# The last output tile of an attention and feed-forward kernel: other column parts, a bank for each, other engines for their copies and sends

## The chip, the core and the metric

The kernel runs on one core of a Trainium2 chip. The metric is the device time of one execution in microseconds; lower is better. A core has a matrix engine (TensorE), three engines for elementwise work (VectorE, ScalarE, GpSimd) and a queue engine (SyncE, SP in the profile). TensorE writes its results to PSUM, an on-chip memory of banks; VectorE or ScalarE copies them from there to SBUF, and a DMA sends them from SBUF to the output in HBM.

## The reference

Linear attention with the feature map phi, and then a gated feed-forward block on its output. Batch is 8, heads 8, sequence 576, head width 64; there are 4608 tokens of width 512, and the hidden width is 1536.

```python
def phi(x):
    return np.where(x > 0, x, np.exp(x) - 1.0) + 1.0

q_p, k_p = phi(q), phi(k)
kv  = einsum('bhsd,bhse->bhde', k_p, v)
z   = sum(k_p, axis=2)
num = einsum('bhsd,bhde->bhse', q_p, kv)
den = einsum('bhsd,bhd->bhs', q_p, z)[..., None] + 1e-06
x   = (num / den), heads side by side: 4608 x 512
g   = x @ w_gate
out = (g * sigmoid(g) * (x @ w_val)) @ w_out          # 4608 x 512, float32
```

## The kernel before

The tokens are worked through in NG = 9 groups of 512. For each group, layer 1 (`l1`, line 292 for the matmuls) makes the hidden activations `hT` in FB = 12 blocks of 128 hidden units: two products into a pair of PSUM banks, a silu on ScalarE and a multiplication on VectorE. Layer 2 then makes the output in four tiles t = 0 to 3 of 128 tokens by 512 columns. Each is a sum over the 12 hidden blocks: `l2_mm` (line 299) is one matmul of that sum, with the weights of one `hT` block loaded and 512 columns of `w_out` streamed. `l2_open` gives the tile its PSUM bank, `l2_out` copies the finished bank to an SBUF tile `osb`, on ScalarE (through the helper at line 120) or on VectorE (line 322), and sends it to HBM in two halves of 64 tokens (line 326), e = 0 and e = 1.

All of PSUM is four pairs of banks, held in the list `ring`. `pair()` takes the pair at the front of the list and puts it at the end, so that a pair comes round again after three others. `l2_open` takes a new pair for tiles 0 and 2; tiles 1 and 3 use the second bank of the pair. The order of the instructions on each engine is the order in which the code issues them. Waits between engines are derived from the tiles and banks that the instructions use. Each queue (SP's, ScalarE's) issues its sends in order.

The last tile, g = 8 and t = 3, is done apart (lines 737 to 744): its 512 columns go in two parts, 0 to 384 and 384 to 512, one after the other, each with its own 12 matmuls. Both parts lie in one bank. The first is copied by VectorE, and both of its halves are sent from SP's queue. The second is copied by ScalarE; its first half is sent from SP's queue and its second half from ScalarE's. The tiles before it are copied by ScalarE (t = 0), VectorE (t = 1) and ScalarE (t = 2), and are sent from SP's queue. At the program's end (line 774) SP waits until all sends have landed.

Of the kernel before, what the change touches and what calls it, by code (L numbers as in the profile page):

```python
# [17 lines left out]
def kernel(  # L18
# [10 lines left out]
    nc = tc.nc  # L29
# [9 lines left out]
    NG = B * J // U  # L39
# [53 lines left out]
    def pair(p=None):  # L93
        i = 0 if p is None else [x is p for x in ring].index(True)
        p = ring.pop(i)
        ring.append(p)
        return p
# [8 lines left out]
    def ld2(src, dst, b):  # L106
        ld(src, dst, b, 0)
        ld(src, dst, b, 1)
# [10 lines left out]
    def act(out, in_, func=AF.Copy, scale=1.0, bias=0.0):  # L119
        nc.scalar.activation(out=out, in_=in_, func=func, bias=bias, scale=scale)  # L120
# [15 lines left out]
    def exp_k(b, lp):  # L136
        act(jl(ek, b, lp), lj(kr, b, lp), AF.Exp)

    def exp_q(b, lp):
        act(eq[b % 2][:, hs(lp), :], qr[b % NB][:, hs(lp), :], AF.Exp)  # L140
# [26 lines left out]
    def phi_k(b, lp):  # L167
        mx_k(b, lp)
        mn_k(b, lp)
        add_k(b, lp)  # L170
# [19 lines left out]
    def kv_all(b):  # L190
        kvp[b] = pair()
        for lp in range(2):
            kv_corner(b, lp, kp, True, True)
# [9 lines left out]
    def zsum(b, l0=0, l1=2):  # L203
        a, z = kp[b % 2][:, l0:l1, :, :], zs[:, l0:l1, :, :]
        nc.vector.tensor_tensor(out=z[:, :, 0:4, :], in0=a[:, :, 0:4, :], in1=a[:, :, 4:8, :], op=ALU.add)
        nc.vector.tensor_tensor(out=z[:, :, 0:2, :], in0=z[:, :, 0:2, :], in1=z[:, :, 2:4, :], op=ALU.add)
        nc.vector.tensor_tensor(out=z[:, :, 0, :], in0=z[:, :, 0, :], in1=z[:, :, 1, :], op=ALU.add)
        nc.vector.tensor_tensor(out=z[:, :, 0, :], in0=z[:, :, 0, :], in1=a[:, :, 8, :], op=ALU.add)
# [31 lines left out]
    def units(g):  # L240
        us = [(u // J, u % J) for u in range(U * g, U * g + U)]
        res = []
        for b in sorted(set(u[0] for u in us)):
            js = [j for (bb, j) in us if bb == b]
            res.append((b, js[0], js[-1] + 1, C * us.index((b, js[0]))))
        return us, res
# [26 lines left out]
    def l1_mm(g, fb, ps, chunks):  # L273
        for c in chunks:
            for h, w in enumerate((wg, wv)):
                nc.tensor.matmul(out=ps[h][:, :], lhsT=w[:, c, P * fb:P * fb + P], rhs=xT[g % 2][:, c, :],  # L276
                                 start=(c == 0), stop=(c == 3))
# [3 lines left out]
    def l1_post(g, fb, ps):  # L281
        s = sil[sn[0] % 4]
        sn[0] += 1
        act(s[:, :], ps[0][:, :], AF.Silu)
        nc.vector.scalar_tensor_tensor(out=hT[g % 2][:, fb, :], in0=ps[1][:, :], scalar=SC,  # L285
                                       in1=s[:, :], op0=ALU.mult, op1=ALU.mult)

    def l1(g, fb):
        ps = pair()
        for h, w in enumerate((wg, wv)):  # L290
            for c in range(4):
                nc.tensor.matmul(out=ps[h][:, :], lhsT=w[:, c, P * fb:P * fb + P], rhs=xT[g % 2][:, c, :],  # L292
                                 start=(c == 0), stop=(c == 3))
        l1_post(g, fb, ps)

    l2p = {}
# [5 lines left out]
    def l2_open(g, t):  # L302
        if t % 2 == 0:
            l2p[(g, "p", t // 2)] = pair()
        l2p[(g, t)] = l2p[(g, "p", t // 2)][t % 2]

    def lay2(g, t):
        l2_open(g, t)
        for fb in range(FB):
            l2_mm(g, t, fb)  # L310
# [3 lines left out]
    def l2_out(g, t, eng, n0=0, n1=512, o=None):  # L314
        if o is None:
            o = osb[on[0] % 4]
            on[0] += 1
        ps = l2p[(g, t)]
        if eng == "A":
            act(o[:, n0:n1], ps[:, n0:n1], scale=1.0 / SC)  # L320
        else:
            nc.vector.tensor_scalar(out=o[:, n0:n1], in0=ps[:, n0:n1], scalar1=1.0 / SC, scalar2=None, op0=ALU.mult)  # L322
        for e in range(2):
            b, j = units(g)[0][2 * t + e]
            dma = nc.scalar if g == NG - 1 and t == 3 and n1 == 512 and e == 1 else nc.sync
            dma.dma_start(out=out[S * b:S * b + S, n0:n1].rearrange("(c j) f -> j c f", j=J)[j],
                              in_=o[C * e:C * e + C, n0:n1])
        return o
# [196 lines left out]
    def none():  # L525
        return [[] for _ in range(FB)], [[] for _ in range(4)]

    def lam(f, *a):
        return lambda: f(*a)
# [19 lines left out]
    def period0():  # L549
        sl, w = none()  # L550
        b = 1
        sl[7] = [lam(mx_k, b, 0), lam(exp_q8), lam(exp_k, b, 0), lam(phi_q8), lam(mn_k, b, 0), lam(add_k, b, 0)]
        sl[8] = [lam(zsum, b, 0, 1)]
        sl[10] = [lam(mx_k, b, 1)]
        return sl

    def chain(b, at):
        return {
            at: [lam(s3_prod, b, 0)],
            at + 1: [lam(s3_reduce, b, 0), lam(s3_recip, b, 0)],  # L560
            at + 2: [lam(s3_scale, b, 0), lam(dtr, b, 0)],
            at + 3: [lam(s3_prod, b, 1)],
            at + 4: [lam(s3_reduce, b, 1), lam(s3_recip, b, 1)],
            at + 5: [lam(s3_scale, b, 1), lam(dtr, b, 1)],
        }
# [102 lines left out]
    for g in range(NG):  # L668
        b1, b2 = g + 1, g + 2
        if g == 0:  # L670
            sl = period0()
        else:
            sl, _ = none()
            late = []
            if g == 1:
                sl[1] = [lam(zsum, b1)]
                sl[4] = [lam(phi_q, b1, 0)]
                sl[5] = [lam(phi_q, b1, 1), lam(zb, b1)]
                ch = chain(b1, 6)
                late = ch.pop(10) + ch.pop(11)  # L680
            elif b1 < B:
                sl[0] = [lam(phi_q, b1, 0)]
                sl[1] = [lam(phi_q, b1, 1)]
                ch = chain(b1, 2)
            else:
                ch = {}
            for f, v_ in ch.items():
                sl[min(f, FB - 1)] += v_
        for fb in range(FB):
            if g == 0:  # L690
                if fb < 2:
                    continue
                if fb == 4:
                    ld2(k, kr, 2)
                    ld2(q, qr, 2)
                    ld2(v, vr, 2)
            if g == 1 and fb < 2:
                if fb == 0:
                    two = [pair(), pair()]
                    for cs in ((0, 1), (2, 3)):  # L700
                        for i in range(2):
                            l1_mm(g, i, two[i], cs)
                l1_post(g, fb, two[fb])
            else:
                l1(g, fb)
            for f in sl[fb]:
                f()
        if g + 3 < B:
            if g > 0:
                nc.gpsimd.tensor_copy(out=gate[:, :], in_=qT[b1 % 2][:, 1, J - 1, 1, C - 1:C])  # L710
            ld2(k, kr, g + 3)
            ld2(v, vr, g + 3)
            if g > 0:
                ld2(q, qr, g + 3)
        if g == 0:
            layer2_0()
            ld2(q, qr, 3)
        else:
            for f in late:
                f()  # L720
            for t in range(4):
                if t == 0 and b2 < B:
                    if g == 1:
                        nc.scalar.preload_act_table_set("natural_log_exp_and_others")
                    exp_k(b2, 0)
                    exp_k(b2, 1)
                    exp_q(b2, 0)
                    exp_q(b2, 1)
                    phi_k(b2, 0)
                    phi_k(b2, 1)  # L730
                    zsum(b2)
                if t == 1 and g == 1:
                    kv_all(b1)
                    r_copy(b1, 0, 2, "AA")
                if t == 3:
                    block(g)
                if g == NG - 1 and t == 3:
                    l2_open(g, t)
                    o = None
                    for (n0, n1) in ((0, 384), (384, 512)):  # L740
                        for fb in range(FB):
                            l2_mm(g, t, fb, n0, n1)
                        o = l2_out(g, t, "V" if n0 == 0 else "A", n0, n1, o)
                    continue
                lay2(g, t)
                l2_out(g, t, "A" if g == 1 and t == 1 else "AV"[t % 2])
            if b2 < B:
                zb(b2)
# [30 lines left out]
```

## Time and profile before

| | |
|---|---|
| median of 5 runs | 313.65 us |
| lowest and highest | 313.54, 313.74 us |
| the profiled execution's own time | 313.54 us |
| its span in the profile | 311.7 us |
| TensorE busy (PE) | 305.0 us, 98% of the span |
| VectorE busy (DVE) | 205.2 us, 66% |
| ScalarE busy (ACT) | 152.6 us, 49% |
| GpSimd busy (POOL) | 48.4 us, 16% |
| granted TensorE clock | full in all slices of the span |

The span goes from the first to the last instruction of the profiled execution; the execution's own time has about 1.8 us more around it. Times in the profile count from the span's start. A line of the timeline has the start, the length, the engine, the source line, the operation and its output and inputs (`osb<-pp` is a copy from a PSUM bank to an output tile), their shapes, and in brackets the idle time of the engine before it and what ended that. SPq and ACTq are the queues from which SyncE and ScalarE issue their sends; the length of such a line is the time of the issue, not of the transfer.

### The profile page before, as it was taken

What the parts mean: (1) busy time and instruction counts of PE and PEld (TensorE: products, weight loads), DVE (VectorE), ACT (ScalarE), POOL (GpSimd) and SP (SyncE); (2) the same over time, 40 slices, a digit from 0 to 9 for tenths busy, and PEclk for the clock granted to TensorE, in tenths of its full rate; (3) what the DMA queues carried; (4) which work ended last, traced back from release to release, by engine and by line L of the source; (5) the groups of instructions that cost most, each with busy time, mean ns of one, the idle gap of its engine ahead of it and who ended that gap; (6) DMA issues with size and microseconds to landing.
All of it is one profiled execution on the core that took longest, in us unless ns stands there. A gap on an engine that the chain in (4) does not pass through costs nothing.

```text
span 311.7 us, 5565 instructions
## 1 busy us (share of the span) xinstructions
PE 305.0 (98%) x2206; PEld 141.7 (45%) x2206; DVE 205.2 (66%) x361; ACT 152.6 (49%) x231; POOL 48.4 (16%) x73
## 2 busy tenths in 40 slices
PE   7999999999999999999999999999999999999994
PEld 3444454444544454445444544454444444444442
DVE  4755868999599658976697759874981433143410
ACT  4865959448733844374536643574330333033311
POOL 8745444400000510041000500000000000000000
PEclk9999999999999999999999999999999999999999
DMA  8999999999502693239512990323032300240014
GB/s 216 199 197 199 206 207 235 235 206 154 114 11 39 103 195 105 40 60 189 154 38 41 129 236 14 62 53 86 0 76 53 84 1 1 46 91 0 2 34 101
DMA packets 41178, 32.80 MB, mean 105 GB/s; under 512 B 16448, under 2 KB 36160, under 8 KB 41152
## 3 DMA queue, kind: packets, MB, share of 16 engines
q0 software_dynamic: 20480, 18.29, 37.5%
q1 hardware_dynamic: 20592, 14.13, 18.9%
q8 instruction: 17, 0.28, 0.4%
q14 instruction: 9, 0.07, 0.1%
q10 hardware_dynamic: 80, 0.03, 0.0%
HBM read 37.75 MB, written 9.44 MB: 151 GB/s over the span
## 4 chain that ended last, share of the span: by engine, by line
PE 95%; DVE 2%; DMA 1%; SPq 0%; issue 0%; ACT 0%; DVEq 0%
PE pp L292 58%; PE pp L299 30%; PE pp L276 2%; PE pp L254 2%; PE pp L185 2%; DMA q<-in_q_dram 1%; DVE qT L454 1%; PE pp L124 1%; DVE xT L425 0%; PE pp L412 0%; PE pp L212 0%; DVE qp L468 0%; PE pp L374 0%; DVE osb L322 0%; SPq L333 0%
## 5 line engine op out<-in xcount | busy, mean ns | idle before, releaser
L120 ACT ACTIVATE sil<-pp 128x512 f16<-128x512 f32 x108 | 63.4, 597 | 101.0 <-PE pp L292 96.4
L292 PE MATMUL pp<-xT,wg 128*128 128x512 f16 x416 | 106.8, 379 | 0.0
L292 PE MATMUL pp<-xT,wv 128*128 128x512 f16 x416 | 106.8, 379 | 0.0
L285 DVE SCALAR_TENSOR_TENSOR hT<-pp,sil 128x512 f16<-128x512 f32 x108 | 72.2, 680 | 48.0 <-PE pp L292 35.4
L299 PE MATMUL pp<-wo,hT 128*128 128x512 f16 (+2 forms) x444 | 97.1, 373 | 0.6 <-DVE osb L322 0.6
L299 PEld LDWEIGHTS <-hT 128*128 128x128 f16 x444 | 41.9, 98 | 49.9 <-issue 2.1
L292 PEld LDWEIGHTS <-wv 128*128 128x128 f16 x416 | 40.7, 98 | 49.1
L292 PEld LDWEIGHTS <-wg 128*128 128x128 f16 x416 | 40.7, 98 | 48.4
L322 DVE TENSOR_SCALAR osb<-pp 128x512 f32<-128x512 f32 (+1 forms) x19 | 12.9, 681 | 31.1 <-PE pp L299 31.1
L120 ACT ACTIVATE osb<-pp 128x512 f32<-128x512 f32 (+1 forms) x18 | 10.3, 574 | 34.8 <-PE pp L299 30.2
L120 ACT ACT_TABLE_LOAD x13 | 16.7, 1283 | 2.5 <-PE pp L292 2.4
L120 ACT ACTIVATE ek<-kr 128x1152 f16<-128x1152 f16 x16 | 17.8, 1157 | 0.1
L229 DVE TENSOR_TENSOR qp<-qp,rden 128x1152 f16<-128x1152 f16 x12 | 16.2, 1346 | 0.0
L220 DVE TENSOR_REDUCE den<-prod 128x18 f32<-128x1152 f16 x12 | 16.1, 1340 | 0.0
L710 POOL COPY gate<-qT 128x1 f16<-128x1 f16 x4 | 1.1, 281 | 96.1 <-DMA qT<-qp 96.1
L120 ACT ACTIVATE eq<-qr 128x1152 f16<-128x1152 f16 x14 | 15.4, 1151 | 0.0
L271 DVE TENSOR_SCALAR xT<-pp 128x512 f16<-128x512 f32 (+1 forms) x14 | 8.8, 667 | 6.7 <-PE pp L254 6.7
L103 POOL DMA_DIRECT2D vr<-in_v_dram x16 | 11.9, 742 | 8.5 <-DMA wo<-in_moe_w_out_dram 2.4
L103 POOL DMA_DIRECT2D kr<-in_k_dram x16 | 11.6, 725 | 8.7 <-DMA wo<-in_moe_w_out_dram 1.9
L159 DVE TENSOR_TENSOR kp<-ek,kp 128x1152 f16<-128x1152 f16 x15 | 11.4, 758 | 0.5
L147 DVE TENSOR_SCALAR ek<-ek 128x1152 f16<-128x1152 f16 x16 | 7.9, 494 | 5.0 <-ACT ek L120 5.0
L103 POOL DMA_DIRECT2D qr<-in_q_dram x14 | 10.1, 721 | 5.3 <-DMA qr<-in_q_dram 2.3
(86 smaller groups left out, 179.5 us busy)
## 6 DMA issues: line engine op xcount, KB each, us to landing
out_dram<-osb SPq DMA_DIRECT2D x70, 128.0 KB, 2.7
kr<-in_k_dram POOLq DMA_DIRECT2D x16, 288.0 KB, 8.6
vr<-in_v_dram POOLq DMA_DIRECT2D x16, 288.0 KB, 9.5
qr<-in_q_dram POOLq DMA_DIRECT2D x14, 288.0 KB, 11.7
wg<-in_moe_w_gate_dram POOLq DMA_DIRECT2D x5, 256.0 KB, 9.4
wv<-in_moe_w_val_dram POOLq DMA_DIRECT2D x5, 256.0 KB, 9.7
q<-in_q_dram SPq DMA_DIRECT2D x2, 576.0 KB, 3.9
wo<-in_moe_w_out_dram POOLq DMA_DIRECT2D x2, 512.0 KB, 12.4
```

Of the source, the lines that this page charges most:

```text
L103: nc.gpsimd.dma_start(out=dst[b % NB][:, 2 * lp:2 * lp + 2, :], in_=src[b].rearrange("(l a) (c j) d -> (a c) l (j d)", a=2, j=J)[:, 2 * lp ...
L120: nc.scalar.activation(out=out, in_=in_, func=func, bias=bias, scale=scale)
L147: nc.vector.tensor_scalar(out=a, in0=a, scalar1=1.0, scalar2=None, op0=ALU.min)
L159: nc.vector.tensor_tensor(out=a, in0=ek[b % 2][:, lp, :, :], in1=a, op=ALU.add)
L185: nc.tensor.matmul(out=ps[hh][D * l2:D * l2 + D, D * lp:D * lp + D], lhsT=t[b % 2][rows, lp, j, D * l2:D * l2 + D], rhs=vr[b % NB][rows, 2 ...
L220: nc.vector.tensor_reduce(out=den[:, c, :], in_=prod[:, :, :].rearrange("p j (l d) -> p (j l) d", d=D), axis=AX.X, op=ALU.add)
L229: nc.vector.tensor_tensor(out=qv, in0=qv, in1=rden[:, c, :].unsqueeze(2).to_broadcast([P, 2 * J, D]), op=ALU.mult)
L271: nc.vector.tensor_scalar(out=dst, in0=ps[l2][:, c0:], scalar1=1.0 / SC, scalar2=None, op0=ALU.mult)
L285: nc.vector.scalar_tensor_tensor(out=hT[g % 2][:, fb, :], in0=ps[1][:, :], scalar=SC, in1=s[:, :], op0=ALU.mult, op1=ALU.mult)
L292: nc.tensor.matmul(out=ps[h][:, :], lhsT=w[:, c, P * fb:P * fb + P], rhs=xT[g % 2][:, c, :], start=(c == 0), stop=(c == 3))
L299: nc.tensor.matmul(out=l2p[(g, t)][:, n0:n1], lhsT=hT[g % 2][:, fb, P * t:P * t + P], rhs=wo[:, fb, n0:n1], start=(fb == 0), stop=(fb == F ...
L322: nc.vector.tensor_scalar(out=o[:, n0:n1], in0=ps[:, n0:n1], scalar1=1.0 / SC, scalar2=None, op0=ALU.mult)
```

## The change

The last tile is cut at column 320 instead of 384. Each part gets its own PSUM bank: after the first part has been copied, the next pair is taken from the list and its first bank is used for the second part. The first part is copied by ScalarE and the second by VectorE, the other way round from before. Of both parts, the first half is sent from SP's queue and the second half from ScalarE's. The assignment of a bank after the second part is not used by anything.

```diff
@@ l2_out @@
         for e in range(2):
             b, j = units(g)[0][2 * t + e]
-            dma = nc.scalar if g == NG - 1 and t == 3 and n1 == 512 and e == 1 else nc.sync
+            dma = nc.scalar if g == NG - 1 and t == 3 and e == 1 else nc.sync
             dma.dma_start(out=out[S * b:S * b + S, n0:n1].rearrange("(c j) f -> j c f", j=J)[j],
                               in_=o[C * e:C * e + C, n0:n1])
@@ the loop over groups @@
                 if g == NG - 1 and t == 3:
                     l2_open(g, t)
                     o = None
-                    for (n0, n1) in ((0, 384), (384, 512)):
+                    for (n0, n1) in ((0, 320), (320, 512)):
                         for fb in range(FB):
                             l2_mm(g, t, fb, n0, n1)
-                        o = l2_out(g, t, "V" if n0 == 0 else "A", n0, n1, o)
+                        o = l2_out(g, t, "A" if n0 == 0 else "V", n0, n1, o)
+                        l2p[(g, t)] = pair()[0]
                     continue
```

## The prediction

> **What bounds the kernel now.** I read the page's chain that ended last first, then the chain in order of time, then the timeline of the last 12 us, then the send queues. On the page, 95% of the chain is TensorE, so only what lengthens the path behind TensorE's last matmuls can matter to this change. The chain in order of time, from 304 us on, shows that path. The columns are start and length in us.
>
> ```profile
> 303.80 3.04 PE pp L299 x17
> 306.84 0.02 issue
> 306.86 0.57 DVE osb L322
> 307.43 0.04 issue
> 307.47 0.84 PE pp L299 x12
> 308.32 0.02 issue
> 308.34 0.28 ACT osb L120
> ```
>
> TensorE works, then waits out a VectorE copy, then does twelve short matmuls, and ScalarE copies their result. The copy in the middle lies on the path although it frees nothing that the matmuls need: they write other columns, but of the same bank. The timeline has the engines side by side (start, length, instruction; in brackets the idle time before it and its releaser).
>
> ```profile
> 302.32 0.69 DVE L322 TENSOR_SCALAR osb<-pp 128x512 f32<-128x512 f32 x1 [4.42 <-PE pp L299]
> 304.91 0.60 ACT L120 ACTIVATE osb<-pp 128x512 f32<-128x512 f32 x1 [4.58 <-PE pp L299]
> 306.86 0.56 DVE L322 TENSOR_SCALAR osb<-pp 128x384 f32<-128x384 f32 x1 [3.85 <-PE pp L299]
> 307.47 0.83 PE L299 MATMUL pp<-wo,hT 128*128 128x128 f16 x12 [0.65 <-DVE osb L322]
> ...
> 308.34 0.28 ACT L120 ACTIVATE osb<-pp 128x128 f32<-128x128 f32 x1 [2.83 <-PE pp L299]
> ```
>
> The 0.65 in the fourth line is TensorE's idle time. A copy starts as soon as its matmuls are through: 302.32, 304.91 and 306.86 are 2.59 us apart for a 512-column tile and 1.95 for the 384-column part.
>
> The end belongs to the sends. The first answer is a narrow timeline at 308.65, the second the DMA issues from 300 us on (size of one, us from issue to landing), the third the waits of SP's queue.
>
> ```profile
> 308.65 0.55 SPq L326 DMA_DIRECT2D out_dram<-osb  x1
> 308.65 0.56 ACTq L326 DMA_DIRECT2D out_dram<-osb  x1
> ```
>
> ```profile
> out_dram<-osb SPq DMA_DIRECT2D x6, 128.0 KB, 2.3
> out_dram<-osb SPq DMA_DIRECT2D x2, 96.0 KB, 2.1
> out_dram<-osb SPq DMA_DIRECT2D x1, 32.0 KB, 1.9
> out_dram<-osb ACTq DMA_DIRECT2D x1, 32.0 KB, 2.1
> ```
>
> ```profile
> SPq L774 <- DMA out_dram<-osb: 1.2, 2, 0.6
> ```
>
> The last two sends leave together at 308.65; the one on ScalarE's queue lands last, at about 310.77, and SP at the program's end waits for landings. From there to the span's end, 311.7, is 0.93 us that the change does not touch.
>
> **The change part by part.** TensorE: the columns stay 512 by 12, but the second part has a bank of its own. The pair of banks that the list gives next was last used for layer 1 of this group, whose last silu copy began at 296.3, so nothing holds it. What a change of bank costs is seen at 304.5 us, where the previous tile's last matmul is followed by this tile's first in the other bank of the pair: the 1.95 to the next copy is just 12 steps of a 384-column matmul (160 ns of streaming at the 512-column pace, and some 2 ns), so the switch is free. The wait of 0.65 us goes. The twelve 128-column matmuls take 0.056 us a step (0.83 less the 0.22 of the last, over 11), so 0.67 for twelve; 1.95 + 0.67 = 2.62 for both parts. I take the same sum for 320 + 192, since the number of matmuls and of columns is the same and the price is linear in columns between these rows. Counted from 304.91, the last copy starts at 307.53 instead of 308.34: **-0.81**.
>
> Last copy: 192 columns on VectorE in place of 128 on ScalarE. VectorE's 512- and 384-column copies of this line took 0.69 and 0.56, which is 1.04 ns a column; 192 fewer than 384 give 0.36. Against 0.28: **+0.08**. The bounds are 0.28 (a 128-column VectorE operation from PSUM elsewhere in this kernel) and 0.56. It ends at 307.89; a send follows a copy by 0.03, so the last pair leaves at 307.92 instead of 308.65: -0.73 so far.
>
> First copy: now ScalarE, 320 columns. Its 128 and 512 columns took 0.28 and 0.60, so 0.44. TensorE finishes part 1 after 12 x 0.136 = 1.63, so the copy runs from 306.54 to 306.98. Its cover is the second part's matmuls and copy (0.99 + 0.36); uncovered it would cost its 0.44, but only if the sends then leave too late, which is next.
>
> Sends of part 1: one stays on SP, one moves to ScalarE's queue, both at 307.01 with 80 KB. SP is free by then: its send before began at 306.05 and took 0.59. Behind ScalarE's send only its own last send is queued. An 80 KB send from this queue is not in the trace; the nearest rows are 0.56 (32 KB, this queue) and 0.59 (96 KB, SP), so it ends at 307.57, and with about 0.09 for the semaphore check and gap that SP shows between its sends the queue is ready at 307.66, 0.26 before 307.92. SP's side is the same or shorter. Cost nothing, with 0.26 of cover. Nothing else moves past a queue, and GpSimd's has nothing there.
>
> Here a rule of the Trainium skill speaks against the change: "DMA: Bandwidth & Descriptors", section "Issuing engines are not separate DMA queues", says that issuing from several engines only saves the sequencer's issue time, usually small beside the transfer. The trace agrees that this is all (0.56 against a 2.1 landing), but here it is what counts: with both part-1 sends on SP the second would start at 307.53 and take 0.59, and SP's last send would leave at 308.21, not 307.92. By the rule read as "worth nothing" the saving would be the same with or without ScalarE's queue; by the rows, 0.29 smaller without.
>
> A second one is "Perfetto Trace Analysis", section "DMA Instruction — HWDGE (DVE, Sync)": descriptors come from one shared block that an issue locks for itself. Two sends issued together would then last 0.47 (the shortest SP row) and 0.47 + 0.56 = 1.03, and two such pairs in a row would put ScalarE's last send at about 309.16, where before it ended at 309.21: with its landing the saving would be gone. But the trace has just this case at 308.65, and the rows are 0.55 and 0.56. I take these; the lock's part is what the ScalarE send lands later, 2.1 against 1.9, and that is in the old time too.
>
> Landing of the last pair: 48 KB each in place of 32. On SP, 96 KB took 0.2 more than 32 KB, so 16 KB add 0.05. If ScalarE's data waits for SP's, as its 0.2 delay suggests, it is up to 0.11. I take **+0.08**, so 2.2; below nothing I leave out, since more bytes do not land sooner, and at most 0.2. The part-1 data (160 KB) should be through at about 309.0, just as the last pair's begins.
>
> Sum: -0.81 + 0.08 + 0.08 = **-0.65**. The profiled execution took 313.54 with a span of 311.7 (1.84 around it), and would take 312.89. It lies 0.11 below the median of 313.65, from which the same difference gives **313.0**.
>
> **The rivals.** (1) The stall is not removed, because the second part waits for the first copy all the same (a bank shared with the first part, or a wait tied to the output tile). TensorE would start part 2 at about 307.03, the copy at 308.22, the sends at 308.61; with the landing this is +0.04, 313.7. The list of pairs speaks against it. 4%.
>
> (2) The issues partly serialise, each ScalarE issue taking 0.75 to 1.0 rather than 0.56. The rule on the shared block is for it, the rows at 308.65 against. At 0.8, ScalarE's queue would be free at 307.90 and its last issue end 0.24 later than forecast: -0.41, 313.24. 9%.
>
> (3) Slower: ScalarE's queue becomes the bound. It now issues twice in a row, each time together with SP. The last landing is 307.01 + X + 0.09 + X + 1.56 (from issue end to landing) + 0.08, X being the length of one issue; it equals the old 310.77 at X = 1.0. The longest issue of this output tile in the trace is 1.43, so such lengths occur; at 1.43 the landing would be 311.6, +0.83, and 314.5. Against it: in the last 12 us no issue is over 0.59. 7%.
>
> **How the numbers follow.** A measurement of this kernel can tell about 0.2%, 0.63 us, from no change. The mechanism as worked out has 80%; its own spread, from landing (0 to 0.2), copy (0.05) and a tenth of a us of scatter, is -0.8 to -0.45, so the line at -0.63 cuts it: 58% beyond, 22% short of it. With rivals 1 and 2, "same" is 35%; rival 3 is the 7% slower. The range 312.85 to 313.35 takes in the mechanism's spread and the nearer half of rival 2, and leaves out rivals 1 and 3 and the outermost scatter.
>
> **What would show it.** Right: TensorE's 192-column matmuls without idle time before them; VectorE's 128x192 copy of 0.36 starting 2.6 us after the previous tile's copy; ScalarE's 128x320 copy of 0.44; two sends on each queue, the last pair 0.73 us earlier measured from the previous tile's copy; landing at 2.2; a span near 311.05. Wrong: 0.6 us of idle time on TensorE between the parts (1), ScalarE issues over 0.7 (2) or over 1.0 (3), or a last landing above 2.4.

## The result and the profile after

| | before | changed |
|---|---|---|
| median, all runs | 313.68 us | 312.85 us |
| ratio, with 95% interval | 1 | 0.9977 [0.9971, 0.9982] |
| span of the profiled execution | 311.74 us | 311.59 us |
| tile 2's copy starts | 304.91 us | 305.51 us |
| from there to the last landing | 5.86 us | 5.11 us |
| from there to the span's end | 6.83 us | 6.08 us |

The ratio is a gain of 0.72 us, with 0.56 to 0.91 as its interval: faster by 0.23%. That is clear of no change, but the interval also takes in 0.2%, the least that the prediction held to be tellable. The two spans alone would hide the gain: this profiled execution reached tile 2's copy 0.60 us later than the one before, and all of that arose in the first 85 us, which the change does not touch. So all traces below are read from the start of ScalarE's copy of tile 2 (the last 128x512 copy on ScalarE). By that clock the changed end is 0.75 us sooner.

The timeline of the last tiles of the changed kernel (lines of tile 2 and of the last tile):

```profile
305.51 0.60 ACT L120 ACTIVATE osb<-pp 128x512 f32<-128x512 f32 x1 [4.58 <-PE pp L299]
307.14 0.44 ACT L120 ACTIVATE osb<-pp 128x320 f32<-128x320 f32 x1 [1.03 <-PE pp L299]
307.61 1.41 ACTq L326 DMA_DIRECT2D out_dram<-osb  x2
308.13 0.36 DVE L322 TENSOR_SCALAR osb<-pp 128x192 f32<-128x192 f32 x1 [4.52 <-PE pp L299]
```

Its chain of waits, in order of time, has lost the copy in the middle:

```profile
303.96 4.14 PE pp L299 x31
308.11 0.02 issue
308.13 0.36 DVE osb L322
```

The narrow timeline of the last pair of sends, and the DMA issues of the last tile (size, us to landing):

```profile
308.51 0.47 SPq L326 DMA_DIRECT2D out_dram<-osb  x1
308.52 0.50 ACTq L326 DMA_DIRECT2D out_dram<-osb  x1
```

```profile
out_dram<-osb SPq DMA_DIRECT2D x1, 80.0 KB, 2.0
out_dram<-osb ACTq DMA_DIRECT2D x1, 80.0 KB, 2.3
out_dram<-osb SPq DMA_DIRECT2D x1, 48.0 KB, 1.8
out_dram<-osb ACTq DMA_DIRECT2D x1, 48.0 KB, 2.1
```

TensorE runs through; the last copy starts 2.62 us after tile 2's (3.43 before), and the last pair leaves at 3.01 (3.74 before).

### The profile page after: what moved, and what is told of

The parts are those of the page before. It is cut to its first block, busy times and chain, and to the rows that moved or that the text cites. A ratio compares the mean times of both kernels' runs of the same rounds, so it can differ in the third digit from the quotient of the medians.

```text
span 311.6 us, 5565 instructions
## 1 busy us (share of the span) xinstructions
PE 305.0 (98%) x2206; PEld 141.9 (46%) x2206; DVE 203.8 (65%) x361; ACT 153.1 (49%) x231; POOL 48.6 (16%) x73
## 4 chain that ended last, share of the span: by engine, by line
PE 86%; DMA 10%; POOL 2%; issue 0%; DVE 0%; POOLq 0%
PE pp L292 52%; PE pp L299 29%; DMA wo<-in_moe_w_out_dram 4%; DMA wg<-in_moe_w_gate_dram 4%; DMA vr<-in_v_dram 3%; PE pp L254 2%; PE pp L185 2%; PE pp L276 1%; POOL kr L103 1%; POOL wv L112 0%; POOL wg L112 0%; POOL vr L103 0%; PE pp L212 0%; PE pp L374 0%; DVE osb L322 0%
```

## The experiments

The table has every kernel that was run. "Sent" is when the later of the last two sends leaves, "landed" the last landing, "end" the span's end, all in us from the start of tile 2's copy.

| kernel | median, its own before | ratio, interval | sent | landed | end |
|---|---|---|---|---|---|
| before | 313.68 | 1 | 3.74 | 5.86 | 6.83 |
| changed | 312.85, 313.68 | 0.9977 [0.9971, 0.9982] | 3.01 | 5.11 | 6.08 |
| bank alone | 313.32, 313.57 | 0.9993 [0.9985, 1.0001] | 3.73 | 5.71 | 6.61 |
| bank and queues | 313.24, 313.57 | 0.9988 [0.9980, 0.9996] | 3.51 | 5.55 | 6.53 |
| part 1 on SP | 312.84, 313.57 | 0.9974 [0.9965, 0.9984] | 3.29 | 5.22 | 6.12 |
| one bank | 313.57, 313.57 | 1.0001 [0.9993, 1.0009] | 3.75 | 5.86 | 6.83 |
| both copies on ScalarE | 312.83, 313.64 | 0.9975 [0.9967, 0.9984] | 3.29 | 5.21 | 6.11 |
| cut at 384 | 313.06, 313.64 | 0.9980 [0.9973, 0.9988] | 3.12 | 5.24 | 6.22 |
| halves exchanged | 313.04, 313.64 | 0.9980 [0.9972, 0.9988] | 3.01 | 5.13 | 6.10 |
| one send for a part | 318.15, 313.64 | 1.0141 [1.0127, 1.0155] | 3.01 | 10.10 | 11.13 |
| three parts, one send each | 318.09, 313.64 | 1.0137 [1.0123, 1.0151] | 2.97 | 10.07 | 11.05 |
| three parts in halves | 313.31, 313.64 | 0.9990 [0.9981, 0.9998] | 2.97 | 5.07 | 6.42 |
| changed, two more sends | 313.31, 313.74 | 0.9986 [0.9979, 0.9992] | 3.01 | 5.15 | 6.48 |
| three in halves, six more sends | 312.90, 313.74 | 0.9976 [0.9967, 0.9984] | 2.97 | 5.08 | 6.07 |

**Without the bank.** My theory was that the bank carries the gain and the rest only lets it through; the rival, that the queues and the other engines carry it.

```diff
--- changed
-                        l2p[(g, t)] = pair()[0]
```

> The changed kernel without the second bank: 320 by ScalarE, 192 by VectorE, both queues, but both parts in one bank. If the bank is what counts, TensorE waits about 0.5 to 0.65 us between the parts, the last sends leave 3.70 us after tile 2's copy and the end is at -0.05 against before. If the queues and the other engines carry the gain, it stays near -0.7 and TensorE's wait is paid for elsewhere.

Nothing of the gain is left (6.83, and a ratio of 1). The lines of TensorE and of the last copy show where it went:

```profile
307.00 1.15 PE L299 MATMUL pp<-wo,hT 128*128 128x192 f16 x12 [0.53 <-ACT osb L120]
308.24 0.36 DVE L322 TENSOR_SCALAR osb<-pp 128x192 f32<-128x192 f32 x1 [5.26 <-PE pp L299]
```

ScalarE's copy has taken the place of VectorE's in front of TensorE. It is also what rival 1 of the prediction described: worked out there as +0.04, measured as 0.01.

**The bank alone.**

```diff
--- before
                         o = l2_out(g, t, "V" if n0 == 0 else "A", n0, n1, o)
+                        l2p[(g, t)] = pair()[0]
```

> The kernel before with only the second bank added: parts 384 and 128, first copied by VectorE and sent by SP, second copied by ScalarE, as before. If the whole gain is TensorE's removed wait, the end moves by about -0.8 us. My theory: the wait goes and ScalarE's copy starts 2.62 us after tile 2's copy instead of 3.43, but SP is still issuing the two sends of part 1 until 3.65 us after that copy, so SP's last send leaves where it left before (3.74 after tile 2's copy) and lands after 1.85; ScalarE's send leaves 0.8 earlier and lands before it. Net -0.27 us against before. If the gain comes from the queues alone, 0.

TensorE's wait is gone and yet only 0.22 us comes out (6.83 to 6.61; the ratio's interval just reaches 1, so the medians alone do not show it). The two copies in its timeline, and a narrow window on the queues:

```profile
307.04 0.56 DVE L322 TENSOR_SCALAR osb<-pp 128x384 f32<-128x384 f32 x1 [3.85 <-PE pp L299]
307.71 0.28 ACT L120 ACTIVATE osb<-pp 128x128 f32<-128x128 f32 x1 [2.02 <-PE pp L299]
```

```profile
308.01 0.57 ACTq L326 DMA_DIRECT2D out_dram<-osb  x1
308.14 1.35 SPq L326 DMA_DIRECT2D out_dram<-osb  x2
```

Part 2 is ready and ScalarE's half leaves at 308.01, but SP is at its second send of part 1 from 308.14 and then at its half of part 2, which leaves where it left before (3.73 after tile 2's copy). The SP queue was a second bound right behind the first. It does not show as a wait in the profile before, where it came free 0.06 us before the last copy ended; only its issue times give it away. Of the 0.22 us, 0.15 is the landing: SP's half, now sent apart from ScalarE's, is last and lands 1.98 after leaving, where before ScalarE's took 2.12. The other 0.07 is the order of SP's checks, explained under the three parts in halves.

**Bank and queues, copies as before.**

```diff
--- before
-            dma = nc.scalar if g == NG - 1 and t == 3 and n1 == 512 and e == 1 else nc.sync
+            dma = nc.scalar if g == NG - 1 and t == 3 and e == 1 else nc.sync
...
+                        l2p[(g, t)] = pair()[0]
```

> The kernel before with the second bank and both parts sent by both queues, but with parts and copies as before (384 by VectorE, 128 by ScalarE). My theory: ScalarE must now issue part 1's send (about 2.54 to 3.10 us after tile 2's copy) before its copy of part 2, which is ready at 2.62; the copy starts at about 3.12, the last sends leave at 3.43, -0.3 us against before. If the swap of the copying engines means nothing, the last sends leave at 2.93 and the gain is -0.8 us.

It gains 0.30 (6.53). SP is relieved, and now ScalarE has to issue part 1's send ahead of its copy of part 2:

```profile
307.45 0.56 ACTq L326 DMA_DIRECT2D out_dram<-osb  x1
308.11 0.28 ACT L120 ACTIVATE osb<-pp 128x128 f32<-128x128 f32 x1 [2.60 <-PE pp L299]
```

The copy starts 3.20 after tile 2's, where part 2 was ready at 2.62. The bracket puts the idle time down to TensorE. That is a trap: an issue is not counted as busy, and TensorE had been done for 0.58 us; what held the copy back was ScalarE's own send, which ended 0.10 before it.

**Part 1 on SP.** The prediction gave ScalarE's queue for part 1 a worth of 0.29 us.

```diff
--- changed
-            dma = nc.scalar if g == NG - 1 and t == 3 and e == 1 else nc.sync
+            dma = nc.scalar if g == NG - 1 and t == 3 and n1 == 512 and e == 1 else nc.sync
```

> The changed kernel, but with both sends of part 1 on SP. The prediction's claim: SP's last send leaves 0.29 us later, and the gain shrinks by as much, to about -0.45 against before. My theory after the result: the ScalarE send of a simultaneous pair lands 0.26 later than SP's, so with the two apart ScalarE's lands first and SP's last send, leaving at 3.30 after tile 2's copy, lands at about 5.23, only 0.12 later than the pair of the changed kernel (5.11): -0.62 against before.

A narrow window on the last pair, and its rows of the DMA issues (size, us to landing):

```profile
308.11 0.56 ACTq L326 DMA_DIRECT2D out_dram<-osb  x1
308.39 0.55 SPq L326 DMA_DIRECT2D out_dram<-osb  x1
```

```profile
out_dram<-osb ACTq DMA_DIRECT2D x1, 48.0 KB, 2.0
out_dram<-osb SPq DMA_DIRECT2D x1, 48.0 KB, 1.9
```

SP's last send does leave 0.28 later, but the landing is only 0.11 later, the end 0.05, and the ratio is that of the changed kernel (0.9974 and 0.9977). The claim falls, for two reasons. A pair that leaves together does not land together: in the changed kernel SP's half landed 1.85 after leaving and ScalarE's 2.10; here, apart, 1.93 and 1.95. So 0.17 of the 0.28 comes back. Another 0.06 comes back at the end, because the half that lands last is now the one that SP checks last (0.90 from landing to end, not 0.96). "Issuing engines are not separate DMA queues" from the page "DMA: Bandwidth & Descriptors" of the Trainium skill was nearer to this than my sum.

**Both copies on ScalarE.**

```diff
--- part 1 on SP
-                        o = l2_out(g, t, "A" if n0 == 0 else "V", n0, n1, o)
+                        o = l2_out(g, t, "A", n0, n1, o)
```

> The changed kernel with both copies on ScalarE and both sends of part 1 on SP. If the last copy has to be on another engine than the first, ScalarE is late for it. My theory: what made ScalarE late in the run with bank and queues was the send that it had to issue ahead of its copy; without one, its second copy starts 2.62 after tile 2's copy like VectorE's, takes 0.33, and SP's last send decides as in the run without ScalarE's queue for part 1: last landing at 5.23, -0.7 against before.

6.11 and 312.83: VectorE isn't needed for the last copy. With the run before this one it shows what is enough: a second bank, and part 1 cut and copied so that its sends leave sooner (2.09 after tile 2's copy against 2.54 in the bank-alone kernel). How much of that is the cut and how much the engine of part 1's copy was not run apart for this kernel.

**Cut at 384.** The cut of the changed kernel is `((0, 320), (320, 512))`; here it is `((0, 384), (384, 512))`.

> The changed kernel cut at column 384 instead of 320. The last copy is shorter (0.29 against 0.36) but the first one later: ScalarE is ready to send at 2.47 after tile 2's copy and its queue free again at about 3.12, so its last send leaves at 3.12 and SP's at 2.94 instead of both at 3.01. Part 1 has 192 KB, which need some 0.95 us of the DMA engines. If the queue decides, the last landing is at 5.1 to 5.15, as in the changed kernel; if the last copy's length decides, 0.07 sooner.

5.24, later than either case. A narrow window on the last pair:

```profile
308.65 0.55 SPq L326 DMA_DIRECT2D out_dram<-osb  x1
308.75 0.73 ACTq L326 DMA_DIRECT2D out_dram<-osb  x1
```

ScalarE's half decides. It left at 3.12 as expected, but only 0.10 after the end of the send before it, and its issue took 0.73, where the changed kernel's took 0.50. SP too had to take its check and gap between two sends (its last left at 3.02, not 2.94), and its 32 KB landed 1.50 after the end of its issue, where 32 KB took 1.30 in the kernel before; part 1's larger data was still on its way (its last half landed at 4.90), which may be why. The shorter copy is paid back. The ratios of the two cuts overlap; only the traces separate them.

This kernel differs from the one with bank and queues only in the engines of the two copies: 6.22 against 6.53. So the swap of the engines brings 0.31, and the cut at 320 another 0.14.

**Halves exchanged.** `e == 1` becomes `e == 0`, so that the first half goes by ScalarE's queue.

> The changed kernel with the queues of the two halves exchanged: first half from ScalarE's queue, second half from SP's. Whichever is second to get its descriptors lands 0.26 later; if that goes by queue, ScalarE's send is again the late one and nothing changes but the order in which SP waits for the landings at the end: if the late one is then waited for last, the span's end is 0.06 nearer to the last landing (0.90 instead of 0.96). Rival: the lag goes with the half, and SP's lands late.

ScalarE's half lands 0.27 after SP's again, so the lag does not go with the half. Whether it goes with the queue or with being second is open: in every such pair here ScalarE's send also began 1 to 5 ns after SP's. The order of SP's checks did not change, and neither did the end (6.10 against 6.08).

**One send for a part, and three parts.** Both halves of a part go as one send of 128 rows, part 1 from ScalarE's queue and part 2 from SP's.

```diff
+        if g == NG - 1 and t == 3:
+            b, j = units(g)[0][2 * t]
+            dma = nc.scalar if n0 == 0 else nc.sync
+            dma.dma_start(out=out[S * b:S * b + S, n0:n1].rearrange("(c j) f -> j c f", j=J)[j:j + 2],
+                          in_=o[:, n0:n1])
+            return o
```

> The changed kernel with one send of 128 rows for each part in place of two of 64: part 1 from ScalarE's queue, part 2 from SP's. If ScalarE's send of a simultaneous pair lands late because its data waits for SP's data, one send of twice the size lands as late: 3.01 after tile 2's copy plus 0.47 for the issue plus the 1.61 that 96 KB took from issue end to landing before, 5.09 against 5.11: no change against the changed kernel. If the lag is that of the second issuer and the data is short beside it, it lands at 4.95 to 5.0, and up to 0.15 us are gained.

Neither: 4.5 us slower. The windows of this kernel (length, busy engines, clock, DMA share, GB/s) and one of the changed kernel:

```profile
309.00:311.00 2.00, 0.00 (x0) 0.00 (x0) 0.00 (x0) 0.00 (x0) 0.00 (x0) 0.86 0.13 31
311.00:313.00 2.00, 0.00 (x0) 0.00 (x0) 0.00 (x0) 0.00 (x0) 0.00 (x0) 0.50 0.12 43
```

```profile
309.00:310.00 1.00, 0.00 (x0) 0.00 (x0) 0.00 (x0) 0.00 (x0) 0.00 (x0) 1.00 0.69 171
```

A DMA share of 0.13 is as much as two of sixteen engines at work. The landings say the same: each of these sends raised its semaphore, the counter that tells of its landing, only twice with data (at 8.24 and 8.30, and at 10.05 and 10.10), where every other send of `osb` raised its own sixteen times. The Trainium skill has the rule ("DMA: Bandwidth & Descriptors", section "Why a DMA increments its semaphore by 16 and not by 1"): a send is spread over the largest number of engines, up to 16, that divides the outermost dimension of both sides. Mine was two halves by 64 rows on the HBM side, so two. The two sends for a part in the changed kernel are not idle duplication.

The same sends with three parts (192, 192 and 128 columns, three banks) fell with it:

> The last tile in three parts of 192, 192 and 128 columns, a bank each, copied by VectorE, ScalarE and VectorE, one send of 128 rows for each part, from SP, ScalarE's queue and SP. From the rows: the parts are ready 0.99, 1.98 and 2.65 us after tile 2's copy; SP sends part 1 at about 1.82 (it is still busy with tile 2), ScalarE part 2 at 2.34, SP part 3 at 2.97; landing 0.47 and about 1.48 later, at 4.92, 0.2 sooner than the changed kernel: -0.9 to -1.0 against before. If the data of the parts piles up on the DMA engines, no better than the changed kernel.

**Three parts in halves.** Parts of 192, 192 and 128 columns, all copied by VectorE, two sends each, and tile 2's second half from ScalarE's queue too.

```diff
--- changed
-            dma = nc.scalar if g == NG - 1 and t == 3 and e == 1 else nc.sync
+            dma = nc.scalar if g == NG - 1 and t >= 2 and e == 1 else nc.sync
...
-                    for (n0, n1) in ((0, 320), (320, 512)):
+                    for (n0, n1) in ((0, 192), (192, 384), (384, 512)):
...
-                        o = l2_out(g, t, "A" if n0 == 0 else "V", n0, n1, o)
+                        o = l2_out(g, t, "V", n0, n1, o)
```

> The changed kernel with three parts (192, 192, 128) in three banks, all copied by VectorE, two sends of 64 rows each, second halves from ScalarE's queue, tile 2's second half too. The queues are then free before each part: parts are ready 0.99, 1.98 and 2.65 us after tile 2's copy, the last copy (0.29) ends at 2.94, the last pair leaves at 2.97, or 3.02 on ScalarE's queue, and lands 2.04 later (32 KB, as in the run with bank and queues): 5.01 to 5.06 against 5.11 of the changed kernel, -0.8 to -0.85 against before. If six sends in 2 us crowd the queues, it is no better than the changed kernel.

It landed about where it was expected, at 5.07, and yet ended at 6.42: 1.35 us after the last landing instead of 0.96. In all these traces a send counts its landing on one of eight semaphores, taken in turn, and at the end SP checks all eight in one fixed order. A check that need not wait takes 0.06 us: here the eight checks start at 5.09, 5.15 and so on to 5.52. In the changed kernel the last pair sits on the seventh and eighth, and ScalarE's half, which lands last, on the seventh, so one check follows the last landing. Here the two sends more have moved the pair to the first and second, and seven follow. (Where SP's half on the eighth lands last, as with the bank alone, part 1 on SP or both copies on ScalarE, none follows: 0.90.) To test this I left the last tile alone and only shifted the turn, by splitting sends of group 7, about 40 us before the end; `t < 1` gives two more sends, and `t < 3`, with the three parts in halves, six:

```diff
--- changed
-            dma.dma_start(out=out[S * b:S * b + S, n0:n1].rearrange("(c j) f -> j c f", j=J)[j],
-                              in_=o[C * e:C * e + C, n0:n1])
+            cuts = (n0, 256, n1) if g == 7 and t < 1 else (n0, n1)
+            for c0, c1 in zip(cuts, cuts[1:]):
+                dma.dma_start(out=out[S * b:S * b + S, c0:c1].rearrange("(c j) f -> j c f", j=J)[j],
+                              in_=o[C * e:C * e + C, c0:c1])
```

> The changed kernel with two more sends long before the end: the first tile of group 7 goes out in four sends (two column halves each) instead of two. Nothing of the last tile is touched. What it tells apart: in the run with three parts and two sends each the last landing was 5.07 us after tile 2's copy, 0.05 sooner than in the changed kernel, yet the span ended 0.35 later. Theory: SP waits at the end for the eight send semaphores in a fixed order, about 0.06 us for each check; sends take the semaphores in turn, two more sends put the last pair on those that SP checks second and third, and six checks (0.37 us) then follow the last landing instead of one. Expected: last landing unchanged at 5.11, span end 0.3 to 0.4 us later, +0.35 against the changed kernel, -0.35 against before. If the crowd of six sends at the end was the cause instead, this kernel is as fast as the changed one.

> The three parts in halves again (192, 192, 128, three banks, VectorE), with six more sends in group 7 (three tiles in two column halves each), so that the turn of the semaphores comes back to where the changed kernel has it. By the theory of SP's order of checks the span now ends 0.96 after the last landing, at 6.03 after tile 2's copy (6.08 in the changed kernel, 6.42 without the six sends): -0.8 against before, and a little under the changed kernel. If crowding at the end was the cause, it stays at 6.4 and -0.35.

SP's waits for landings (us in total, times, longest) in the changed kernel, and in the changed kernel with two more sends:

```profile
SPq L775 <- DMA out_dram<-osb: 1.2, 2, 0.6
```

```profile
SPq L777 <- DMA out_dram<-osb: 1.6, 1, 1.6
```

In the first SP waits twice, the second time for the last landing near the end of its list; in the second it waits once, at the head of the list, and has the rest still to check. Two sends more at an earlier place cost 0.40 us at the end with the landing nearly unchanged (5.15; end 6.48). The expectation had the last pair on the second and third semaphores and six checks behind the last landing; it was the first and second, and seven, so six more than in the changed kernel. Six more sends bring the turn round, and the three parts end at 6.07. Both came out as the theory said in the main, and against crowding. The end is then 0.01 from the changed kernel's: no version here beats it by what can be told.

## Why the prediction was right, and where it was not

The forecast was -0.65 us and 313.0; the trace shows -0.75, the ratio -0.72, the medians -0.83. The measured median, 312.85, is the lower edge of the range, so the range held with nothing to spare. The mechanism, TensorE's wait gone and the sends close behind, is what the trace shows.

- *TensorE's wait goes, -0.81.* Right to 0.01: the last copy starts 2.62 after tile 2's. The change of bank is free, and the linear price of columns holds: 0.136 and 0.082 us a step for 320 and 192 columns. Without the second bank nothing of the gain is left; with the bank alone only 0.22 comes out, so the queues and the copies are needed for the rest.
- *Last copy +0.08.* Right: 0.36. First copy 0.44 as worked out, and covered.
- *Sends of part 1 cost nothing.* Right as to ScalarE's issue (0.56) and the cover (its last send did not wait). Wrong as to what the second queue is worth: 0.05 at the span's end, not 0.29. The step took it that what leaves 0.29 later lands and ends 0.29 later; the lag of a simultaneous pair ate 0.17 of it and the order of SP's checks 0.06. Nothing in the sum rested on it.
- *Landing +0.08.* The mis-sized term: measured -0.02 (2.12 before, 2.10 after). The data did take longer, from the end of the issue to the landing 1.38 against 1.30 on SP's queue and 1.61 against 1.56 on ScalarE's. But the issue became shorter: 0.47 against 0.55 on SP, where the queue now had a pause of 0.45 before it in place of 0.09, and 0.50 against 0.56 on ScalarE. ScalarE's lands last, so its 0.06 is what counts. In the kernel before, that send was the first from ScalarE's queue, and here it is the second, after a pause of 0.36; the first takes 0.56 in the changed kernel too. Why the first takes longer is open. The prediction compared whole landings, did not split them at the end of the issue, and left out anything below nothing. This is the 0.1 by which the trace beats the sum.
- *The lag as SP's data.* Wrong: I allowed up to 0.11 for ScalarE's half waiting behind SP's bytes. It lags by 0.27, 0.26 and 0.24 with 32, 48 and 80 KB, so it does not grow with the size there.
- *0.93 after the last landing, untouched.* 0.97 before and 0.96 after. True here, since the change keeps the number of sends and ScalarE's half still lands last; the three parts in halves show that it need not be.
- *Rivals.* In the changed kernel the issues did not serialise: 0.56 and 0.50 on ScalarE's queue. Lengths close to those of rival 2 (0.75 to 1.0) do occur where this queue has a shorter pause: 0.73 with the cut at 384 (pause 0.10), 0.63 and 0.78 with the three parts in halves (0.20 and 0.11). No full wait for the lock of the shared descriptor block shows in the rows of a simultaneous pair (0.47 and 0.50); whether the lock makes the lag was not settled.

## What to carry to other kernels

A wait at the end of a kernel is worth taking away only if the next thing behind it is also ready: here a free bank brings 0.22 us alone and 0.75 once the earlier sends are out of the way. Before costing a tail, write out each queue with its issue times, and look at what an engine must issue ahead of its own next copy: the profile can put that idle time down to another engine. Read tails from a common event near the end, since profiled executions can differ at the start by as much as the change: tile 2's copy starts between 304.88 and 305.70 in the traces here.

## What the hardware showed that I had not expected

- Two sends issued at the same time from SP and ScalarE landed 0.24 to 0.29 us apart at 32 to 96 KB, and 0.32 to 0.36 at 128 KB, ScalarE's later each time; with 0.28 between their issues, each took 1.93 to 1.95.
- In the last 12 us of these traces, the issue of a send of 64 rows on SP's queue took 0.47 us after a pause of 0.28 or more, 0.55 after 0.09 (once 0.67) and 0.59 after 0.05: after the two short pauses, pause and length came to 0.64 together, so a send right behind another did not end sooner by starting sooner. On ScalarE's queue the first issue took 0.56, later ones 0.50 after a pause of 0.35 or more and 0.63 to 0.78 after 0.10 to 0.20.
- From the end of SP's issue to the landing, at the end of the kernel before and of the changed one: 1.30 us at 32 KB, 1.38 at 48, 1.58 at 80, 1.61 at 96, 1.76 to 1.79 at 128.
- Sends whose outermost dimension was 2 landed as from two of the sixteen engines: 31 to 47 GB/s, and 4.5 us on the whole kernel.
- Which semaphores the last sends happen to use is worth up to 0.4 us, at 0.06 for each check that comes after the last landing.
